# Both heads of an attention unit turned by VectorE, values in mid-step, and the last batch's remainder first

## The chip, the cores and the metric

The kernel runs on one core of a Trainium2 chip. The metric is the time of one execution on the device, in microseconds (us). The core's engines work side by side[...]: TensorE (PE; its weight loads are listed apart as PEld), VectorE (DVE), ScalarE (ACT), GpSimd (POOL), and SyncE (SP), whose queue issues nearly all transfers. Each engine takes its instructions in the order in which the program lists them.

## The reference

Eight batches, eight heads, 576 positions, head dimension 64, all in fp32. Attention keeps the 32 largest scores of every row, and a two-layer network with a normalisation follows on 512 channels:

```python
scores = scale * q @ k^T                      # (B, H, 576, 576)
kth    = 32nd largest of each row
attn   = softmax(scores where scores >= kth, else -1e9)
x      = attn @ v, heads side by side         # (B, 576, 512)
xn     = (x - mean) / sqrt(var + 1e-6) * g_ln
out    = x + relu(xn @ w_ch1) @ w_ch2         # 512 -> 2048 -> 512
```

The two weight matrices arrive as 64-bit floats and are turned to fp32 in the kernel.

## The kernel before, in words

**Units, groups, jobs.** Two heads are worked on together (a head pair, `hp`). A row of 576 positions is cut into four tiles of 128 query rows and a rest of 64. A *unit* is one tile of one head pair, with both heads' rows (two tiles of 128 x 576 scores), or the rest, in which both heads share one tile of 128 rows. There are 160 units: 128 full, 32 rests. A *group* is the units whose results are multiplied with the values in one go, `[0,1]`, `[2,3]`, or with the rest `J` added; a *job* is one group list of one batch and head pair. From batch 2 on a batch has the jobs `[0,1,J]` for its four head pairs, then `[2,3]` for them.

**Steps.** The order is written out by hand: one loop over `n` (line 900) is a step, in which several units stand at different stages. In step n, VectorE selects the top 32 of unit n (`select`, four pieces 0 to 3), while TensorE makes the scores of unit n+1 (`scores`, L354, copied from PSUM by ScalarE in L335), ScalarE masks unit n-1 (`mask`, L442) and exponentiates unit n-2 (`weigh`, L452). Unit n-2 is then *turned*: its weights, queries on partitions, are needed with keys on partitions. The group whose last unit is n-3 is multiplied with the values (`values`, L563 and L570), and `place` transposes the result (L602) and scales it by the reciprocal denominators (L932, L579). Scores live in four buffers used in turn (`scpool`), exponentials in two, the turned weights (`pt`) in one.

**Selection.** A maximum of eight (MAX8) followed by a replacement of those eight (MATCH_REPLACE8), four rounds. From unit 8 on (`EARLY`) units are *halved*: columns i and i + 288 are compared, the larger goes to `hi`, the smaller to `lo`; the 16 largest of `lo` join `hi`, and the four rounds run on 304 columns rather than 576. VectorE makes `hi` (L376); GpSimd makes `lo` as (a + b) - hi on the bit patterns, in L375 and L377. The first eight units run their rounds on whole rows (L416, L423).

**Turning.** Usually four TensorE transposes a head (L505) and a ScalarE copy to `pt` (L517, L521), and one transpose for the last 64 columns of both heads (L538). In 72 units (`moved`: full units from batch 2 on that are not the last of their group) head 1 goes another way: VectorE transposes it in blocks of 32 x 32 (L482) into the unit's own score buffer, one transfer writes that to HBM (L487), and four transfers read it back so that the blocks land on the right partitions of `pt` (L489). `move` stands near the start of the step, after the first piece of the selection.

**The network.** When the x rows of a job list are complete, they become a *block* of two or three tiles of 128 rows (`gives` says at which step). Its work is a list of small TensorE items: transposes of x (L667), the hidden products (L680), the projections (L697). `fill()`, called at eight places of a step, pops items in order, as many as the step's `share` allows; `slot(n)` computes the share so that only `RESERVE` is left when the next block is given. What is left after the last step runs at the end. `dve_cost` and `pe_cost` are the planner's own estimates of a step.

**Start.** Until about unit 16 the weights are converted: ScalarE and GpSimd split and join the 64-bit words, VectorE shifts (L188). `prepare` makes the exponential's bias, on VectorE in this stage (L436, L437) and on GpSimd later.

Of the kernel before, what the change touches and what calls it, by code (L numbers as in the profile page):

```python
# [16 lines left out]
TOP_K = 32  # L17
# [4 lines left out]
J = 4  # L22
# [7 lines left out]
def kernel(  # L30
# [277 lines left out]
    class Unit:  # L308
        def __init__(self, job, group, qt):
            self.job, self.group, self.qt = job, group, qt  # L310
            self.rest = qt == J
            self.tiles = [(0, 1)] if self.rest else [(0,), (1,)]

            self.moved = False

            self.halved = False
            self.e = None
            self.weighed = 0
# [44 lines left out]
    def halve(u):  # L363

        nt = len(u.tiles)  # L370
        u.lo = lopool.tile([P, 2, HALF], FP32, tag="lo", name="lo")
        u.hi = hipool.tile([P, 2, HALF + TOP_K // 2], FP32, tag="hi", name="hi")
        a, b = u.sc[:, 0:nt, 0:HALF], u.sc[:, 0:nt, HALF:S]
        lo, hi = u.lo[:, 0:nt], u.hi[:, 0:nt, 0:HALF]
        nc.gpsimd.tensor_tensor(lo.bitcast(I32), a.bitcast(I32), b.bitcast(I32), ALU.add)  # L375
        nc.vector.tensor_tensor(hi, a, b, ALU.max)  # L376
        nc.gpsimd.tensor_tensor(  # L377
            lo.bitcast(I32), lo.bitcast(I32), hi.bitcast(I32), ALU.subtract
        )

    def select_halved(u, i):
        nt = range(len(u.tiles))
# [22 lines left out]

    def select(u, i):

        if u.halved:
            return select_halved(u, i)
        nt = range(len(u.tiles))  # L410
        if i == 0:
            u.cur = [u.sc[:, t] for t in nt]
            u.wk = {}
        m = small.tile([P, 2, 8], FP32, tag=f"m{i}", name=f"m{i}")
        for t in nt:
            nc.vector.max(m[:, t, :], u.cur[t])  # L416
        if i < TOP_K // 8 - 1:
            for t in nt:
                if i == 0:

                    o = (NF - 4 + 2 * t) * DM
                    u.wk[t] = w2[:].rearrange("p f n -> p (f n)")[:, o : o + S]
                nc.vector.match_replace(u.wk[t], m[:, t, :], u.cur[t], LOWEST)  # L423
                u.cur[t] = u.wk[t]
        if i == 0:
            u.top = m
        u.thr = m

    def prepare(u):

        nt = len(u.tiles)
        u.bias = small.tile([P, 2], FP32, tag="bias", name="bias")
        b = u.bias[:, 0:nt]

        engine = nc.vector if u.i < CONVERTING else nc.gpsimd
        engine.tensor_tensor(b, u.thr[:, 0:nt, 7], u.top[:, 0:nt, 0], ALU.subtract)  # L436
        engine.tensor_scalar(b, b, scale, 0.0, ALU.mult, ALU.add)  # L437

# [27 lines left out]
    def place_of(u):  # L466

        g = u.group  # L470
        if g.pt is None:
            g.pt = ptpool.tile([P, 2 * J + 1, GQ], FP32, tag="pt", name="pt")
            g.ptB = g.pt[:, J : 2 * J].rearrange("p c n -> p (c n)").rearrange(
                "p (i c n) -> p i c n", c=J, n=32
            )
        return sum(P for x in g.qts if x < u.qt)

    def move(u):

        i0 = place_of(u) // 32  # L480
        t = u.sc[:, 1, 0:JP]
        nc.vector.transpose(  # L482
            t.rearrange("p (j c n) -> p j c n", j=P // 32, c=J),
            u.e[:, 1, R:S].rearrange("p (c j k) -> p j c k", c=J, k=32),
        )
        hbm = hbmpool.tile([P, JP], FP32, tag="turned", name="turned")
        nc.sync.dma_start(hbm[:], t)  # L487
        for j in range(P // 32):
            nc.sync.dma_start(  # L489
                u.group.ptB[j * 32 : (j + 1) * 32, i0 : i0 + P // 32].rearrange(  # L490
                    "k i c n -> k i (c n)"
                ),
                hbm[:, j * P : (j + 1) * P].rearrange("(i k) x -> k i x", k=32),
            )

    def turn(u):

        g = u.group
        q0 = place_of(u)
        i0 = q0 // 32  # L500

        def part(t):
            ps = turned()
            for c in range(J):
                nc.tensor.transpose(  # L505
                    ps[:, c * P : (c + 1) * P], u.e[:, t, c * P + t * R : (c + 1) * P + t * R],
                    ident[:],
                )
            if u.rest:
                both = ps[:].rearrange("p (c h n) -> p h c n", h=2, n=R)  # L510
                nc.scalar.copy(g.pt[:, 0:J, q0 : q0 + R], both[:, 0])
                nc.scalar.copy(
                    g.ptB[:, i0 : i0 + R // 32],
                    both[:, 1].rearrange("p c (i n) -> p i c n", n=32),
                )
            elif t == 0:
                nc.scalar.copy(  # L517
                    g.pt[:, 0:J, q0 : q0 + P], ps[:].rearrange("p (c n) -> p c n", n=P)
                )
            else:  # L520
                nc.scalar.copy(  # L521
                    g.ptB[:, i0 : i0 + P // 32],
                    ps[:].rearrange("p (c i n) -> p i c n", c=J, n=32),
                )
# [15 lines left out]

        heads = [0] if u.moved else range(len(u.tiles))
        return [lambda t=t: part(t) for t in heads] + [last]
# [15 lines left out]
    def values(g):  # L558
        vb = g.job.v
        av = brief("av")  # L560
        for c in range(J):
            for h in range(2):
                nc.tensor.matmul(  # L563
                    av[h * D : (h + 1) * D, 0 : g.nq],
                    vb[:, h * J + c, :],
                    g.ptB[:, 0 : g.nq // 32, c, :] if h else g.pt[:, c, 0 : g.nq],
                    start=(c == 0),
# [179 lines left out]
    for b in range(B):  # L747
        parts = [[0, 1], [2, 3], [J]]
        if b:
            parts = [[0, 1], [2, 3]]  # L750
            parts[b < 2].append(J)
        for qts in parts:
# [22 lines left out]
    EARLY = jobs[NHP].first  # L775
    for u in units[EARLY:]:
        u.halved = True

# [36 lines left out]
    SLOTS = 8  # L815
    RESERVE = 4.0
    last_give = max(gives)
# [9 lines left out]

    DVE_UNIT, DVE_REST, DVE_HALVED, DVE_MOVE = 10.3, 5.3, 0.9, 0.8

# [6 lines left out]
    def pe_cost(n):  # L836
# [4 lines left out]
        if ex:  # L841
            c += 0.67 if ex.rest else 0.55 if ex.moved else 1.0
        if g:
# [3 lines left out]
    def dve_cost(n):  # L847
        u, ex = at(n), after(n)[0]
        c = 5.0 if u is None else DVE_REST if u.rest else DVE_UNIT
        if u and u.halved:  # L850
            c *= DVE_HALVED
        return c + DVE_MOVE if ex and ex.moved else c

    def give(n):
# [9 lines left out]
    def slot(n):  # L864


        if n <= CONVERTING:
            return max(0.0, dve_cost(n) - pe_cost(n)) / SLOTS
        left = sum(t[1] for t in todo)
        if n > last_give:  # L870
            even = left / max(1, END - 1 - n)
        else:
            even = 99.0
            for m in sorted(gives):
                if m > n:
                    even = min(even, (left - RESERVE) / (m - n))
                    left += sum(b.cost() for b in gives[m])
        return max(0.0, even) / SLOTS

# [15 lines left out]
    load(fresh[1], nc.sync, nc.scalar)  # L895
    scores(units[0])
    load_gain()
    weights(-1, 0)
    weights(-1, 1)
    for n in range(END):  # L900
# [14 lines left out]
        moved = ex is not None and ex.moved  # L915
        order = (1, 0) if moved else (0, 1)
        sent, stores[:] = stores[:], []

        if ex and not early:
            weigh(ex, order[0])  # L920
        if nxt:
            scores(nxt)
        if g:
            values(g)
        if u:
            select(u, 0)
        if moved:
            move(ex)
        for store in sent:
            store()  # L930
        for den in recips.pop(n, []):
            nc.vector.reciprocal(den, den)  # L932
        if n == gives_first:
# [11 lines left out]
        if ex and len(ex.tiles) > 1 and not early:  # L945
            weigh(ex, order[1])
        fill()
        if parts and not moved:
            parts[0]()
        if ex and ex.rest:  # L950
            keep_den(ex)
        if u:
            select(u, 1)
        if nxt and nxt.halved:
            halve(nxt)
        if n in turns:
            turn_heads(turns[n])
            later = fresh.index(turns[n]) + 1
            if later < len(fresh):
                load(fresh[later], nc.sync, nc.sync)  # L960
        for blk, i in rows_of.pop(n, []):
            blk.stats(i)
        if not quick:
            weights(n, 1)
        fill()
        if mk and not early:
            mask(mk, int(mk.moved))
        if g:
# [4 lines left out]
        fill()  # L973
        if moved:
            parts[0]()
        elif len(parts) > 2:
            parts[1]()
        if u:
            select(u, 2)
        for blk in gives.get(n - 2, []):  # L980
            blk.inverse()
# [10 lines left out]
        if mk and len(mk.tiles) > 1 and not early:  # L992
            mask(mk, 1 - int(mk.moved))
        fill()
# [11 lines left out]
        if u:  # L1006
            select(u, 3)
            if u.i < CONVERTING:
                prepare(u)
        for x in (g, quick):  # L1010
            if x and x.job.hp == NHP - 1:
# [44 lines left out]
```

## Time and profile before

Three runs: 1665.63, 1666.67 and 1667.17 us. The profiled execution has a span of 1666.8 us.

| engine | busy us | share | instructions |
|---|---|---|---|
| TensorE | 1574.1 | 94% | 7113 |
| VectorE | 1464.5 | 88% | 4476 |
| ScalarE | 1077.2 | 65% | 2759 |
| GpSimd | 664.0 | 40% | 879 |

| what | line | count | mean us | busy us |
|---|---|---|---|---|
| projections | L697 | 1152 | 0.599 | 546.1 |
| hidden products | L680 | 2048 | 0.411 | 550.0 |
| transposes of weights | L505 | 864 | 0.285 | 138.1 |
| maxima of halves | L376 | 152 | 0.913 | 138.8 |
| POOL's two passes | L375, L377 | 304 | 1.3 | 394.5 |
| VectorE's move | L482 | 72 | 0.698 | 50.3 |
| write to HBM, 256 KB | L487 | 72 | 2.0 to landing | |
| read back, 64 KB | L489 | 288 | 2.0 to landing | |

Records of TensorE overlap, so busy time is less than count times mean. In the views used below, a line of the timeline has start, length, engine, source line, operation, tile written and read, shapes and count; the square bracket is idle time before it and what ended it. A line of stretches has the busy time of PE, PEld, DVE, ACT and POOL, then the granted clock of TensorE, the share of the transfer engines and GB/s. A line of waits says who waited for whom, in us, how often, and the longest.

### The profile page before, as it was taken

What the parts mean: (1) busy time and instruction counts of PE and PEld (TensorE: products, weight loads), DVE (VectorE), ACT (ScalarE), POOL (GpSimd) and SP (SyncE); (2) the same over time, 40 slices, a digit from 0 to 9 for tenths busy, and PEclk for the clock granted to TensorE, in tenths of its full rate; (3) what the DMA queues carried; (4) which work ended last, traced back from release to release, by engine and by line L of the source; (5) the groups of instructions that cost most, each with busy time, mean ns of one, the idle gap of its engine ahead of it and who ended that gap; (6) DMA issues with size and microseconds to landing.
All of it is one profiled execution on the core that took longest, in us unless ns stands there. A gap on an engine that the chain in (4) does not pass through costs nothing.

```text
span 1666.8 us, 25284 instructions
## 1 busy us (share of the span) xinstructions
PE 1574.1 (94%) x7113; PEld 955.1 (57%) x7113; DVE 1464.5 (88%) x4476; ACT 1077.2 (65%) x2759; POOL 664.0 (40%) x879
## 2 busy tenths in 40 slices
PE   3568989989999999999999999999999999999998
PEld 1346556566555575755547575745547575755564
DVE  5998999999999999999999999899998999998000
ACT  5677967767666776767666675767666676665310
POOL 5567854343433434343343434343243433333010
PEclk9758999999999999999999999999999999999999
DMA  7423333001331133213231233112331132111000
GB/s 176 100 64 108 89 58 59 22 14 27 76 81 51 53 76 81 65 54 69 59 86 51 55 73 83 52 54 70 65 89 44 53 81 74 52 46 47 26 13 13
DMA packets 301203, 104.58 MB, mean 63 GB/s; under 512 B 246276, under 2 KB 283144, under 8 KB 301064
## 3 DMA queue, kind: packets, MB, share of 16 engines
q1 hardware_dynamic: 296328, 102.39, 24.4%
q10 hardware_dynamic: 4736, 0.59, 0.3%
q8 instruction: 57, 0.93, 0.2%
q14 instruction: 82, 0.67, 0.1%
HBM read 74.58 MB, written 28.31 MB: 62 GB/s over the span
## 4 chain that ended last, share of the span: by engine, by line
PE 71%; DVE 21%; issue 4%; ACT 2%; POOL 1%; DMA 1%; ACTq 0%; POOLq 0%; DVEq 0%; SPq 0%
PE hps L680 25%; PE ops L697 24%; PE scps L354 8%; PE av L563 6%; DVE m L398 5%; DVE hi L385 4%; PE tp L505 4%; DVE hi L390 2%; DVE m L416 2%; PE av L570 2%; DVE w L423 2%; DVE lo L385 1%; DVE hi L376 1%; DVE size L188 1%; PE tp L667 1%
## 5 line engine op out<-in xcount | busy, mean ns | idle before, releaser
L680 PE MATMUL hps<-xT,w 128*128 128x256 f32 (+1 forms) x2048 | 550.0, 411 | 2.7 <-ACT xT L672 2.3
L697 PE MATMUL ops<-w,h 128*128 128x512 f32 x1152 | 546.1, 599 | 0.0
L398 DVE MAX8 m<-hi 128x8 f32<-128x304 f32 x1088 | 460.7, 458 | 2.3
L680 PEld LDWEIGHTS hps<-xT,w 128*128 128x128 f32 x2048 | 372.1, 191 | 108.5 <-issue 17.3
L385 DVE MATCH_REPLACE8 hi<-m,hi 128x304 f32<-128x304 f32 x816 | 368.0, 456 | 0.0
L375 POOL TENSOR_TENSOR lo<-sc 128x576 int32<-128x576 int32 (+1 forms) x152 | 197.7, 1301 | 316.3 <-ACT sc L335 156.9
L697 PEld LDWEIGHTS ops<-w,h 128*128 128x128 f32 x1152 | 200.2, 191 | 169.9 <-issue 164.6
L377 POOL TENSOR_TENSOR lo<-lo,hi 128x576 int32<-128x576 int32 (+1 forms) x152 | 196.8, 1295 | 141.9 <-DVE hi L376 139.7
L354 PE MATMUL scps<-kT,qT 64*128 64x288 f32 (+3 forms) x1344 | 217.4, 433 | 32.4 <-DVE qT L304 20.9
L335 ACT COPY sc<-scps 128x288 f32<-128x288 f32 x576 | 199.2, 409 | 62.3 <-PE scps L354 51.0
L442 ACT ACTIVATE e<-sc,m 128x576 f32<-128x576 f32 x288 | 224.3, 779 | 9.7 <-DVE m L398 6.2
L452 ACT ACTIVATE e<-e,bias 128x576 f32<-128x576 f32 x288 | 224.6, 780 | 2.9 <-DVE bias L437 2.5
L390 DVE MAX8 hi<-lo 128x8 f32<-128x288 f32 x544 | 221.8, 443 | 2.6 <-POOL lo L377 1.5
L354 PEld LDWEIGHTS scps<-kT,qT 64*128 64x128 f32 (+1 forms) x1344 | 122.4, 181 | 146.6 <-issue 56.2
L505 PEld LDWEIGHTS tp<-ident,e 128*128 128x128 f32 x864 | 110.9, 147 | 115.9 <-ACT e L452 51.7
L505 PE MATMUL tp<-ident,e 128*128 128x128 f32 x864 | 138.1, 285 | 38.2 <-ACT e L452 37.9
L692 ACT ACTIVATE h<-hps 128x256 f32<-128x256 f32 (+1 forms) x256 | 105.9, 414 | 96.5 <-PE hps L680 93.8
L436 POOL TENSOR_TENSOR bias<-m,m 128x2 f32<-128x2 f32 (+1 forms) x143 | 27.8, 195 | 303.6 <-DVE m L398 303.6
L563 PE MATMUL av<-pt,vb 128*64 128x256 f32 (+2 forms) x1088 | 146.7, 413 | 0.0
L376 DVE TENSOR_TENSOR hi<-sc 128x576 f32<-128x576 f32 (+1 forms) x152 | 138.8, 913 | 5.5 <-ACT sc L335 5.5
L385 DVE MATCH_REPLACE8 lo<-hi,lo 128x288 f32<-128x288 f32 x272 | 118.2, 440 | 0.0
L517 ACT COPY pt<-tp 128x512 f32<-128x512 f32 x128 | 74.6, 583 | 62.1 <-PE tp L505 60.5
(79 smaller groups left out, 1295.0 us busy)
## 6 DMA issues: line engine op xcount, KB each, us to landing
turned<-sc SPq DMA_DIRECT2D x72, 256.0 KB, 2.0
pt<-turned SPq DMA_DIRECT2D x288, 64.0 KB, 2.0
vb<-in_v_dram SPq DMA_DIRECT2D x136, 128.0 KB, 2.5
raw<-in_moe_w_ch_dram SPq DMA_DIRECT2D x32, 512.0 KB, 4.0
kin<-in_k_dram SPq DMA_DIRECT2D x128, 72.0 KB, 2.5
qin<-in_q_dram SPq DMA_DIRECT2D x120, 72.0 KB, 2.5
out_dram<-o SPq DMA_DIRECT2D x32, 256.0 KB, 2.2
ends<-in_v_dram SPq DMA_DIRECT2D x136, 16.0 KB, 2.2
```

The costliest lines, as they stand in the source:

```text
L335: nc.scalar.copy(u.sc[:, t, s * HALF : (s + 1) * HALF], made[s][t][:, 0:HALF])
L354: nc.tensor.matmul(ps[i * R : i * R + ql, o : o + width], qT[r, q0 : q0 + ql], kT[r, k0 : k0 + width], start=True, stop=True,)
L375: nc.gpsimd.tensor_tensor(lo.bitcast(I32), a.bitcast(I32), b.bitcast(I32), ALU.add)
L385: nc.vector.match_replace(x[:, t], m[:, t, :], x[:, t], LOWEST)
L390: nc.vector.max(u.hi[:, t, o : o + 8], u.lo[:, t])
L398: nc.vector.max(m[:, t, :], u.hi[:, t])
L442: nc.scalar.activation(u.e[:, t], u.sc[:, t], AF.Prelu, bias=u.thr[:, t, 7:8], scale=-1.0, alpha=SLOPE)
L452: nc.scalar.activation(u.e[:, t], u.e[:, t], AF.Exp, bias=u.bias[:, t : t + 1], scale=-scale / SLOPE, accum_out=g.den[:, col : col + 1],)
L505: nc.tensor.transpose(ps[:, c * P : (c + 1) * P], u.e[:, t, c * P + t * R : (c + 1) * P + t * R], ident[:],)
L563: nc.tensor.matmul(av[h * D : (h + 1) * D, 0 : g.nq], vb[:, h * J + c, :], g.ptB[:, 0 : g.nq // 32, c, :] if h else g.pt[:, c, 0 : g.nq], ...
L680: nc.tensor.matmul(ps["h"][:, 0:N], w1[:, c, f * P : (f + 1) * P], xT[0][:, c, 0:N], start=(c == 0), stop=(c == NC - 1),)
L697: nc.tensor.matmul(ps[i][:], hT[f][:, i * P : (i + 1) * P], w2[:, f, :], start=(f == 0), stop=(f == NF - 1),)
```

## The change

1. `move` now turns both heads of a moved unit: two VectorE transposes, one transfer of 512 KB to HBM, four transfers back whose runs are 1 KB rather than 512 B. `pt` holds both heads in blocks of 32 queries for this. No head of a moved unit is turned on TensorE; only the last 64 columns are. `move` stands at the end of the step.
2. `values` moves from the start of the step to its middle, the reciprocals of the denominators from the start to after the halving.
3. Every unit is halved, and GpSimd's two passes are (a - hi) + b, so both follow VectorE's maximum.
4. In the converting stage the bias is one VectorE instruction a tile rather than two a unit.
5. The last batch has the jobs `[J]`, `[0,1]`, `[2,3]`, so its rest is worked first and makes a block of one tile. With that, 68 units are moved.
6. The planner: new cost figures, a reserve of 7 rather than 4, and a share proportional to VectorE's cost around the step. Rows' statistics (L629) run later in the step. Moved units mask and weigh head 0 first, as others do.

```diff
@@ halve
-        nc.gpsimd.tensor_tensor(lo.bitcast(I32), a.bitcast(I32), b.bitcast(I32), ALU.add)
         nc.vector.tensor_tensor(hi, a, b, ALU.max)
         nc.gpsimd.tensor_tensor(
-            lo.bitcast(I32), lo.bitcast(I32), hi.bitcast(I32), ALU.subtract
+            lo.bitcast(I32), a.bitcast(I32), hi.bitcast(I32), ALU.subtract
         )
+        nc.gpsimd.tensor_tensor(lo.bitcast(I32), lo.bitcast(I32), b.bitcast(I32), ALU.add)
@@ prepare
-        engine = nc.vector if u.i < CONVERTING else nc.gpsimd
-        engine.tensor_tensor(b, u.thr[:, 0:nt, 7], u.top[:, 0:nt, 0], ALU.subtract)
-        engine.tensor_scalar(b, b, scale, 0.0, ALU.mult, ALU.add)
+        if u.i < CONVERTING:
+            for t in range(nt):
+                nc.vector.tensor_scalar(
+                    b[:, t : t + 1], u.thr[:, t, 7:8], u.top[:, t, 0:1], scale,
+                    ALU.subtract, ALU.mult,
+                )
+            return
...
@@ move
-        t = u.sc[:, 1, 0:JP]
-        nc.vector.transpose(...)
-        hbm = hbmpool.tile([P, JP], FP32, tag="turned", name="turned")
-        nc.sync.dma_start(hbm[:], t)
+        blocks = u.sc[:].rearrange("p t n -> p (t n)")[:, 0 : 2 * JP]
+        for t in range(2):
+            nc.vector.transpose(
+                blocks.rearrange("p (j t c n) -> p j t c n", j=ni, t=2, c=J)[:, :, t],
+                u.e[:, t, t * R : t * R + JP].rearrange("p (c j k) -> p j c k", c=J, k=32),
+            )
+        hbm = hbmpool.tile([P, 2 * JP], FP32, tag="turned", name="turned")
+        nc.sync.dma_start(hbm[:], blocks)
+        for j in range(ni):
...
+                hbm[:, j * 2 * P : (j + 1) * 2 * P].rearrange("(i k) x -> k i x", k=32),
@@ turn
-        heads = [0] if u.moved else range(len(u.tiles))
+        heads = () if u.moved else range(len(u.tiles))
@@ jobs
             parts = [[0, 1], [2, 3]]
-            parts[b < 2].append(J)
+            if b == B - 1:
+                parts = [[J]] + parts
+            else:
+                parts[b < 2].append(J)
@@ planner
-    for u in units[EARLY:]:
-        u.halved = True
-    RESERVE = 4.0
+    RESERVE = 7.0
-    DVE_UNIT, DVE_REST, DVE_HALVED, DVE_MOVE = 10.3, 5.3, 0.9, 0.8
+    DVE_UNIT, DVE_REST, DVE_MOVE, DVE_TURN = 8.6, 5.0, 1.4, 1.45
+        return max(0.0, ratio * pace(n) - pe_cost(n)) / SLOTS
@@ the step
-        if g:
-            values(g)
         if u:
             select(u, 0)
-        if moved:
-            move(ex)
...
-        for den in recips.pop(n, []):
-            nc.vector.reciprocal(den, den)
...
         fill()
+        if g:
+            values(g)
         if parts and not moved:
             parts[0]()
...
         if u:
             select(u, 1)
-        if nxt and nxt.halved:
+        if nxt:
             halve(nxt)
+        for den in recips.pop(n, []):
+            nc.vector.reciprocal(den, den)
...
             select(u, 3)
             if u.i < CONVERTING:
                 prepare(u)
+        if moved:
+            move(ex)
```

## The prediction

> **What bounds the kernel now.** I read the page's slices first, then four stretches, then the waits of VectorE (DVE), then the timeline of PE and DVE.
>
> ```profile
> PE   3568989989999999999999999999999999999998
> ...
> DVE  5998999999999999999999999899998999998000
> ```
>
> Each digit is a busy share in tenths of 41.7 us. In the first eleven slices (to some 458 us) PE has gaps, and DVE hardly any after the first. Then both are full, and DVE stops at about 1542 us while PE works on to the end. Start, us, span, then PE, PEld, DVE, ACT, POOL busy:
>
> ```profile
> 0.00:458.00 458.00, 372.69 (x1788) 235.47 (x1789) 431.15 (x1248) 328.89 (x824) 246.72 (x288) 0.91 0.30 72
> 458.00:1338.00 880.00, 878.16 (x3986) 522.77 (x3986) 842.44 (x2631) 589.36 (x1528) 335.18 (x474) 1.00 0.26 65
> 1338.00:1542.00 204.00, 203.45 (x940) 128.00 (x937) 187.53 (x590) 131.03 (x344) 72.76 (x105) 1.00 0.22 59
> 1542.00:1667.00 125.00, 119.80 (x404) 68.85 (x403) 3.42 (x10) 27.94 (x65) 9.34 (x13) 1.00 0.06 18
> ```
>
> Early (0 to 458) is DVE's: PE idles 85 us. In the middle (batches 2 to 6) PE idles 1.8 us of 880 and DVE 37.6. The end (last batch and tail, 329 us) is PE's. What DVE waits for:
>
> ```profile
> DVE sc L482 <- ACT e L452: 59.4, 19, 13.4
> ```
>
> The move (L482) stands early in its step and waits for an exponential, which follows PE; this is DVE's whole slack. Is PE dense, or only marked busy?
>
> ```profile
> 1443.43 0.60 PE L505 MATMUL tp<-ident,e 128*128 128x128 f32 x4
> ...
> 1604.67 1.04 PE L667 MATMUL tp<-ident,x 128*128 128x128 f32 x8
> ...
> 1606.44 27.89 PE L680 MATMUL hps<-xT,w 128*128 128x256 f32 x128
> 1634.17 27.63 PE L697 MATMUL ops<-w,h 128*128 128x512 f32 x64
> ```
>
> Dense: 64 records in 27.63 us are 0.432 us each, and between 458 us and the end starts of L697 stand 0.440 us apart on average. Four more transposes cost 1.04 - 0.60 = 0.44 us, 0.11 each. A block of two tiles costs PE 1.04 + 27.9 + 27.6 = 56.6 us.
>
> **What the Trainium skill says.** "Perfetto Trace Analysis", Identifying the Most-Contended Engine, calls matmul busy share a poor measure of TensorE; hence the spacing above, which here agrees with the busy share. "SBUF — State Buffer", SBUF: two separate sides: a VectorE instruction with two SBUF inputs and a GpSimd instruction exclude each other for a whole instruction, and the second blocks. The trace agrees:
>
> ```profile
> 1111.09 1.41 POOL L375 TENSOR_TENSOR lo<-sc 128x576 int32<-128x576 int32 x1 [3.22 <-ACT sc L335]
> ...
> 1111.21 1.90 DVE L376 TENSOR_TENSOR hi<-sc 128x576 f32<-128x576 f32 x1
> ...
> 1502.40 0.75 DVE L376 TENSOR_TENSOR hi<-sc 128x576 f32<-128x576 f32 x1
> ```
>
> Begun 0.12 us into POOL's add, the maximum takes 1.90 us; alone, 0.75. "VectorE: DVE Perf Modes", The three transpose paths: VectorE transposes only 32x32 blocks, so the rest of the turn has to be transfers, as here.
>
> **The change, part by part.**
>
> *PE.* 72 units lose head 1's transposes already; now 68 (12 in each of batches 2 to 6, 8 in the last, where [0,1] no longer contains the rest) lose head 0's too. In the middle 57 moves x 4 x 0.11 = -25 us: 855 us of PE work are left. The copies behind them (L517, 0.583 us each on ACT) go as well; ACT is at 67% there, worth nothing by itself.
>
> *DVE, transposes.* L482 runs 72 times at 0.698 us; now 136. Middle: +57 x 0.694 = +39.6 us.
>
> *DVE, halving.* POOL now subtracts only after DVE's maximum, so POOL's first pass can no longer hold the port against it. In the middle L376 is 94 instructions with 88.6 us; 75 full ones at 0.746 and 19 half ones at 0.445 would be 64.4. -24.2 us. Lower bound of the gain: a third, if other POOL work (L638, L710) takes its place; upper: all. I take all, since those ran before, too. The price: both POOL passes (2 x 1.41) follow the maximum. What waits for them is the next step's first maxima of lo; between lie the last two selects (about 4.0 us), so about 1 us is left, and 1.4 more in moved steps. Zero, at most 10 us in all from late POOL queues.
>
> Middle sum for DVE: 842.4 - 24.2 + 39.6 = 858 us, PE 855. Two engines of equal load where there were 880 and 842.
>
> *The move's new place.* At the end of the step its exponentials are long done: the wait at L482 (30.7 us of it in the middle) goes. But the next step's scores go into the same score buffer (four buffers, unit n+1 on that of n-3), and now must wait until the 512 KB have left it. Before, almost a whole step lay between. Counted from the transposes' end:
>
> ```profile
> 1450.49 0.69 DVE L482 STREAM_TRANSPOSE sc<-e 128x512 f32<-128x512 f32 x1
> ...
> 1451.21 0.35 SPq L487 DMA_DIRECT2D turned<-sc  x1
> ...
> 1453.39 1.76 SPq L489 DMA_DIRECT2D pt<-turned  x4
> ```
>
> The readback waits for the landing, 2.2 us after the issue. Each of 16 engines moves eight packets; those of 2 KB took 0.089 us, those of 4 KB (weights) 0.159 median, 0.213 mean, so 512 KB land 0.6 to 1.0 us later: 2.6 to 3.0 us after issue. Then ACT's four copies (1.3 to 1.5 us): scores stand at 3.9 to 4.5 us. DVE wants them at L376, 3.93 us into its step (on the timeline a step's first maximum of lo starts at 1507.91, its L376 at 1511.84). Stall 0 to 0.6 us a move; with ACT ready I take 0.2: 57 x 0.2 = 11 us. Queued behind on ACT are relus (L692), for which three PSUM buffers stand between, so PE runs on. On SP the move follows the loads and the value loads of its step and stands ahead of the next stores; the four readbacks (before 1.76 us to issue) must land before values two steps later, over 10 us: nothing. 1 KB runs make their packets half as many per byte; the doubled bytes raise DMA from 26% to some 35%: nothing.
>
> *Values in mid-step.* Price between 0 and 0.6 us a group: PE's xo transposes need ACT's copy of av (0.43 us), and now only one filler slot lies between rather than three. A slot gives 0.5 to 0.9 us of work. I take 0.05 x 64 = 3 us. Reciprocals after L376 wait for nothing and stand before place: 0.
>
> *Early stage.* Eight units halved: whole rows take 4 x 1.33 + 3 x 1.45 = 9.7 us (pairs of L416 and L423 on the timeline), halved 2.3 + 5.6 + 0.75 = 8.6: -8 us, as DVE binds. POOL gains 8 x 2.85 us in a stage where it is half busy; from -8 to +6 if the joins of weights slip. The bias in one instruction a tile: L436/L437 on DVE have 10.7 + 1.1 + 3.1 us; a fused small one is not shown, 0.17 to 0.67 us by nearest rows: -9 to +7, I take -4. Port: -4 after 208 us. Three moves: +2. Sum about -13, and I take -12.
>
> *End.* The last batch's rest comes first: its block is one tile alone. With 128 columns, 64 hidden products are 128 records; at 0.155 us estimated (256 columns took 0.218, weights' loads 0.191) against 0.107 as share of three tiles: +6 us (0 to +11). Four groups more in values: +3. 16 fewer transposes: -2. The new reserve of 7 leaves 3 us to the end at most. What PE has left when DVE ends shrinks from 3/7 of three tiles (36 us) + 56.6 to some 15 (three short steps and the reserve) + 56.6, but PE is full either way, so only its sum counts: +8.
>
> **The sum.** Middle: DVE 858 + 11 of stall + 3 for values = 872, -8. Early -12, end +8. 1666.8 - 12 - 8 + 8 = 1654.8, so 1655. The profiled span is 1666.8, the runs' median 1666.67, so no shift.
>
> **Rivals.**
> - *PE stays the bound and all its saving shows.* For: gap-free starts before, DVE's slack of 37.6 us. Against: DVE at 858 of 858. Middle 858: 1666.8 - 12 - 22 + 8 = 1641.
> - *The score buffer decides (slower).* At 0.55 us a move the middle is 858 + 31 + 3 = 892, and 1666.8 - 12 + 12 + 8 = 1675; break-even is 0.4 us, and a landing as late as the 512 KB weight loads' (4.0 us on the page, a read) makes it 1.4 us: 1723. For: the 4 KB packets' upper figure, and any other transfer in flight; against: writes of 256 KB were steady at 2.0. Taken at 0.7 us: 1683.
> - *No change.* The place of values costs PE 0.3 us in 56 groups, 17 us, and eats the rest: 1666. Against: ACT waited for av 64 times (119 us), so it is early.
> - *The change does not do what it says*: it can't well, as the transposes at PE vanish with the code; only four of 72 moves go.
>
> **How the numbers follow.** Forecast 0.46, first rival 0.22, second 0.19, third 0.13. Under 0.2% (3.3 us) no difference can be told here. Faster: 0.41 + 0.22 + 0.05 = 0.68. Same: 0.04 + 0.06 = 0.10. Slower: 0.01 + 0.19 + 0.02 = 0.22. The likeliest by itself spans 1643 to 1666; the range, 1630 to 1682, takes in the first rival with 11 us more from the early stage, and about half of the second.
>
> **What would show it.** L505 at some 610 records; L482 136 times, without a wait. L376 at 0.75 us throughout. Middle: DVE over 98% with PE idle 10 us or more (forecast), or PE gap-free (first rival). Second rival: DVE waits at L376 for ACT's sc, and ACT at L335 for the transfer of sc, tens of us. Third: PE idle at L602 for oT. Wrong in the early stage: L390 waiting for POOL's lo.

## The result, and the profile after

The changed kernel takes 1676.31 us (median of four runs, 1676.14 to 1677.18); the kernel before, on the same chip, 1666.92 (1665.63 to 1667.95). The ratio is 1.0058, 95% interval 1.0040 to 1.0075: 9.4 us slower, where 1655 was forecast. The profiled execution spans 1675.4 us.

Line numbers are those of the kernel that a view is of. In the changed kernel the scores are L352 and their copies L333, the maximum of the halves L373, GpSimd's passes L374 and L377, the move L466 with its write L471 and readback L474, the transposes of the weights L488, the values L542 and L549, the copy of their result (`oT`) L554, its transpose in `place` (`xo`) L581, the statistics of the x rows L608, their centring L617, and their transposes for a block L646.

The slices again, on the page of the changed kernel:

```profile
PE   2569989899899999999999999999999999999998
...
DVE  5998999999999999999999999998889878889500
```

TensorE looks as full as before. VectorE, which was at 9 in nearly every slice until it stopped at 1542 us, has slices of 8 and 7 from the 28th on (1130 us), and stops later. The four stretches with the edges of the prediction (columns as there):

```profile
0.00:458.00 458.00, 364.78 (x1751) 227.71 (x1751) 426.12 (x1328) 325.93 (x817) 269.63 (x302) 0.90 0.31 74
458.00:1338.00 880.00, 871.62 (x3754) 500.25 (x3754) 834.76 (x2620) 545.51 (x1445) 329.49 (x468) 1.00 0.35 97
1338.00:1542.00 204.00, 201.63 (x1043) 130.09 (x1043) 174.76 (x557) 126.45 (x343) 68.73 (x101) 1.00 0.28 72
1542.00:1676.00 134.00, 127.21 (x514) 82.80 (x510) 33.84 (x108) 44.08 (x113) 19.70 (x27) 0.99 0.12 38
```

In the same 880 us of the middle, PE has 8.4 us idle rather than 1.8. VectorE has fallen to 834.8 busy, 95%; only short stretches are full (31.00 of 31 us from 552 on). Its waits, largest first, and the one for GpSimd's `lo`:

```profile
DVE hi L373 <- ACT sc L333: 79.7, 55, 5.8
DVE hi L389 <- POOL lo L377: 13.1, 12, 3.0
```

The first is the wait that the second rival named. But 55 us of it lie in the last two batches, and most of that comes with the new order of the last batch: 47 us there with the old planner, 19 with the old order (experiments 6 and 7), none with the new planner alone on the kernel before (experiment 9). PE's own waits:

```profile
PE tp L488 <- ACT e L434: 35.6, 14, 10.8
...
PE tp L646 <- POOL x L617: 13.2, 8, 5.2
PE xo L581 <- ACT oT L554: 12.7, 14, 2.8
PE tp L646 <- POOL r L617: 9.1, 2, 7.4
```

The first is the start (37.9 before). The other three were 5.3, 0.5 and 0.

**Where the time went.** I cut the trace at the first score product of each batch, and priced every TensorE record at the closest spacing of its kind (a projection 0.429 us, a hidden product of 256 columns 0.216, of 128 columns 0.111, a transpose 0.109): that is TensorE's *own work*. The rest of a batch's length is *lost*: waits, changes of tile shape (some 0.2 us where hidden products follow scores, in batch 4), a lower granted clock. Before / after, us:

| batch | length | own work | lost |
|---|---|---|---|
| 0 and 1 | 391.4 / 384.4 | 252.1 / 248.7 | 139.2 / 135.6 |
| 2 | 182.4 / 191.1 | 168.8 / 164.4 | 13.6 / 26.6 |
| 3 | 188.7 / 191.8 | 177.8 / 173.7 | 10.9 / 18.1 |
| 4 | 188.3 / 186.5 | 179.5 / 174.0 | 8.9 / 12.5 |
| 5 | 190.2 / 191.5 | 179.7 / 178.6 | 10.4 / 12.9 |
| 6 | 188.5 / 212.1 | 179.7 / 196.6 | 8.9 / 15.4 |
| 7 and tail | 329.2 / 310.0 | 312.3 / 287.0 | 16.8 / 23.0 |

Own work fell by 27 us in all, and what is lost rose by 35. Batch 2 lost most. Two stretches of it, and the row that PE waits for:

```profile
424.00:456.00 32.00, 24.21 (x84) 12.14 (x85) 31.31 (x96) 15.58 (x42) 12.36 (x20) 0.84 0.37 102
456.00:488.00 32.00, 32.00 (x137) 17.30 (x136) 26.39 (x81) 18.86 (x48) 12.59 (x18) 1.00 0.38 102
```

```profile
447.45 0.69 DVE L608 BATCH_NORM_STATS2 st<-r 128x6 f32<-128x512 f32 x1
...
448.74 0.70 POOL L617 TENSOR_SCALAR r<-r,less 128x512 f32<-128x512 f32 x1
...
449.49 1.11 PE L646 MATMUL tp<-ident,r 128*128 128x128 f32 x4 [7.41 <-POOL r L617]
```

PE has run out of work of the earlier block; the first row of the next one gets its statistics late (L608), is centred late (L617), and PE stands still for 7.4 us. The granted clock in these 32 us is 0.84. In the kernel before, PE was busy for 29.8 us of the same 32, at 0.95.

### The profile page after: what moved, and what is told of

It reads as the page before. It is cut to its first block, busy times and chain, and to the rows that moved or that the text cites. A ratio compares the mean times of both kernels' runs of the same rounds, so it can differ in the third digit from the quotient of the medians.

```text
span 1675.4 us, 25027 instructions
## 1 busy us (share of the span) xinstructions
PE 1565.2 (93%) x7057; PEld 940.8 (56%) x7057; DVE 1469.5 (88%) x4611; ACT 1042.0 (62%) x2715; POOL 687.5 (41%) x897
## 4 chain that ended last, share of the span: by engine, by line
PE 61%; DVE 27%; issue 5%; POOL 4%; ACT 2%; DMA 1%; ACTq 0%; POOLq 0%; DVEq 0%
PE hps L659 22%; PE ops L676 21%; DVE m L397 8%; DVE hi L384 7%; PE scps L352 7%; PE av L542 5%; DVE hi L389 4%; DVE lo L384 2%; DVE hi L373 2%; PE tp L488 2%; PE av L549 2%; DVE size L188 1%; POOL lo L374 1%; POOL lo L377 1%; PE tp L646 1%
## 5 line engine op out<-in xcount | busy, mean ns | idle before, releaser
L659 PE MATMUL hps<-xT,w 128*128 128x256 f32 (+2 forms) x2176 | 551.2, 397 | 2.4 <-ACT xT L651 1.9
L397 DVE MAX8 m<-hi 128x8 f32<-128x304 f32 x1152 | 489.7, 462 | 3.3
L374 POOL TENSOR_TENSOR lo<-sc,hi 128x576 int32<-128x576 int32 (+1 forms) x160 | 209.2, 1307 | 587.7 <-DVE hi L373 298.8
L389 DVE MAX8 hi<-lo 128x8 f32<-128x288 f32 x576 | 234.4, 444 | 14.2 <-POOL lo L377 13.1
L333 ACT COPY sc<-scps 128x288 f32<-128x288 f32 x576 | 198.6, 411 | 70.9 <-PE scps L352 49.2
L352 PE MATMUL scps<-kT,qT 64*128 64x288 f32 (+3 forms) x1344 | 217.2, 431 | 25.4 <-DVE qT L304 22.1
L377 POOL TENSOR_TENSOR lo<-lo,sc 128x576 int32<-128x576 int32 (+1 forms) x160 | 206.7, 1292 | 12.6
L352 PEld LDWEIGHTS scps<-kT,qT 64*128 64x128 f32 (+1 forms) x1344 | 121.9, 180 | 134.4 <-issue 69.0
L373 DVE TENSOR_TENSOR hi<-sc 128x576 f32<-128x576 f32 (+1 forms) x160 | 115.6, 723 | 79.8 <-ACT sc L333 79.7
L671 ACT ACTIVATE h<-hps 128x256 f32<-128x256 f32 (+2 forms) x272 | 109.1, 402 | 100.3 <-PE hps L659 98.4
L542 PE MATMUL av<-pt,vb 128*64 128x256 f32 (+2 forms) x1152 | 146.2, 397 | 0.0
L488 PE MATMUL tp<-ident,e 128*128 128x128 f32 x608 | 97.1, 285 | 35.6 <-ACT e L434 35.6
L488 PEld LDWEIGHTS tp<-ident,e 128*128 128x128 f32 x608 | 77.9, 148 | 83.4 <-ACT e L434 44.4
L542 PEld LDWEIGHTS av<-pt,vb 128*64 128x64 f32 x1152 | 75.2, 141 | 75.9 <-ACT sc L333 22.2
L554 ACT COPY oT<-av 128x256 f32<-128x256 f32 (+2 forms) x72 | 26.9, 374 | 139.3 <-PE av L549 139.2
```

The costliest lines, as they stand in the source:

```text
L352: nc.tensor.matmul(ps[i * R : i * R + ql, o : o + width], qT[r, q0 : q0 + ql], kT[r, k0 : k0 + width], start=True, stop=True,)
L374: nc.gpsimd.tensor_tensor(lo.bitcast(I32), a.bitcast(I32), hi.bitcast(I32), ALU.subtract)
L377: nc.gpsimd.tensor_tensor(lo.bitcast(I32), lo.bitcast(I32), b.bitcast(I32), ALU.add)
L389: nc.vector.max(u.hi[:, t, o : o + 8], u.lo[:, t])
L397: nc.vector.max(m[:, t, :], u.hi[:, t])
L488: nc.tensor.transpose(ps[:, c * P : (c + 1) * P], u.e[:, t, c * P + t * R : (c + 1) * P + t * R], ident[:],)
```

## The experiments

Every ratio is against the kernel before on the same chip, with its 95% interval; "us" is the ratio's difference from 1 times 1666.9, so the changed kernel stands at +9.7. Most intervals are 1 to 2 us to either side.

**1. POOL's passes behind the maximum, alone.** Kernel before plus:

```diff
-        nc.gpsimd.tensor_tensor(lo.bitcast(I32), a.bitcast(I32), b.bitcast(I32), ALU.add)
         nc.vector.tensor_tensor(hi, a, b, ALU.max)
-            lo.bitcast(I32), lo.bitcast(I32), hi.bitcast(I32), ALU.subtract
+            lo.bitcast(I32), a.bitcast(I32), hi.bitcast(I32), ALU.subtract
+        nc.gpsimd.tensor_tensor(lo.bitcast(I32), lo.bitcast(I32), b.bitcast(I32), ALU.add)
```

> The kernel before with one edit: GpSimd's two passes as (a - hi) + b, both behind VectorE's maximum. Theory (VectorE's port wait is what the middle of the changed kernel lives on, but TensorE is the bound before): L376 falls from 139 to about 104 us, yet the time falls only by what VectorE-bound stretches between 208 and 458 us give, 0 to 5 us: 1662 to 1667. Rival (VectorE bounds the middle already): some 20 us faster, 1645. Rival (the later GpSimd pass makes the next step's maxima wait): slower, over 1670, with L390 waiting for lo by tens of us.

1.0012 [1.0006, 1.0019], +2.0 us. Two groups of it (busy us, mean ns, idle time before it):

```profile
L375 DVE TENSOR_TENSOR hi<-sc 128x576 f32<-128x576 f32 x120 | 93.6, 780 | 7.1 <-ACT sc L335 6.6
...
L482 DVE STREAM_TRANSPOSE sc<-e 128x512 f32<-128x512 f32 x72 | 50.4, 701 | 71.9 <-ACT e L452 71.6
```

The maximum falls from 124.6 to 93.6 us, as forecast, and the wait at the move grows from 59.4 to 71.9. Batches 3 to 6 take the same time as before to 0.1 us. VectorE's time is worth nothing there: TensorE sets the pace.

**2 and 3. Both heads moved at the step's end; then with edit 1 too.** Kernel before plus (cut):

```diff
+        for t in range(2):
+            nc.vector.transpose(...)
-        heads = [0] if u.moved else range(len(u.tiles))
+        heads = () if u.moved else range(len(u.tiles))
-        if moved:
-            move(ex)
...
+        if moved:
+            move(ex)
```

> The kernel before with one edit: both heads of the 72 moved units turned by VectorE, the move at the end of the step; values, halving, job order and planner as before. Theory (VectorE becomes the bound): middle 842 + 40 = 882 us of VectorE work against 880 before, so no gain and some stalls: 1667 to 1680. Rival (TensorE stays the bound): its 29 us show, 1640. Rival (the score buffer's handover decides): VectorE waits at L376 for sc by 30 us or more and the time is over 1685.

> The kernel before with both edits together: GpSimd's passes behind the maximum, and both heads moved at the end of the step; early units, values, job order and planner as before. Theory (the middle's sum of 858 for VectorE against 855 for TensorE holds, and the changed kernel lost it again in the early stage and at the end): 1650 to 1660. Rival (the two edits are themselves the loss, by the handover of buffers): 1670 or more, like the changed kernel's 1676.

1.0028 [1.0017, 1.0040] and 1.0034 [1.0022, 1.0046]: +4.7 and +5.7 us. The heart of the change, with only what belongs to it (the layout of `pt`, head 0 masked first, 0.15 us as the planner's price of such a unit on TensorE), makes the kernel slower; the second expectation missed. In the second kernel PE waits for the readback before its values (there L560) 14 times, 24.3 us (experiment 10). In the first, batch 2 takes 188.7 us with some 25 lost, almost as much as in the changed kernel.

**4. First eight units on whole rows again.** Changed kernel, less halving of the first eight units:

```diff
+        if u.i < EARLY:
+            return select_whole(u, i)
...
-        if nxt:
+        if nxt and nxt.i >= EARLY:
             halve(nxt)
```

> The changed kernel, with the first eight units selected on whole rows again. Theory (the early stage gained nothing since GpSimd's 23 us of halving came in the way of the weights' joins): L188 falls back from 28 to about 18 us and the time to 1664 to 1673. Rival (early halving is worth its 8 us of VectorE and something else took the early gain): 1680 to 1686.

1.0043 [1.0031, 1.0055], +7.2 us. That overlaps the changed kernel's interval, so the runs alone show no gain. The profiles agree with a small one: batch 0 takes 209.7 us rather than 213.2 (210.5 to 216.6 in the eight profiles here with early halving), the later batches differ by half a us at most. VectorE's shift of the 64-bit words, in the kernel before, the changed one and this one:

```profile
L188 DVE TENSOR_SCALAR size<-size 128x512 uint32<-128x512 uint32 x32 | 17.8, 590 | 7.3 <-POOL size L185 7.3
```

```profile
L188 DVE TENSOR_SCALAR size<-size 128x512 uint32<-128x512 uint32 x32 | 28.2, 915 | 2.9 <-POOL size L185 2.9
```

```profile
L188 DVE TENSOR_SCALAR size<-size 128x512 uint32<-128x512 uint32 x32 | 19.3, 640 | 6.5 <-POOL size L185 6.5
```

Same instruction, same count: from 0.59 to 0.92 us when POOL halves eight more units, and back to 0.64 without that. Undisturbed it takes 0.39. On the timeline of the changed kernel it lasts 1.62 to 1.64 us seven times, each time begun 0.1 to 0.3 us into a pass of POOL's halving that itself takes some 1.5, and ends 0.3 us after it. Early halving costs VectorE 9 us here (28.2 - 19.3; 5 to 9 over the eight profiles) in waits of this kind, which the prediction didn't count.

**5. One of the two VectorE transposes left out.** Changed kernel; head 0 isn't transposed in `move`, so that part of its weights is left uncomputed:

```diff
-        for t in range(2):
+        for t in (1,):
```

> The changed kernel without head 0's VectorE transposes in the 68 moves (that head's turned weights are then stale data; the transfers stay as they are). Theory (in batches 2 to 5 VectorE is the bound, and what it pays for the turn eats TensorE's saving): 68 x 0.69 = 46 us of VectorE go, batches 2 to 5 fall from 761 us to about TensorE's floor of 4 x 183 = 732, the time to 1640 to 1655. Rival (the handover of the score buffer or the transfers bound the steps, not VectorE's work): no more than 10 us faster, 1666 or more.

1.0012 [1.0004, 1.0020]: 7.6 us less than the changed kernel, for 68 x 0.68 = 46 us less work on VectorE. Batches 4 and 5, of the changed kernel and then of this one:

```profile
775.00:962.00 187.00, 185.86 (x794) 103.33 (x794) 183.28 (x576) 117.86 (x311) 70.23 (x100) 1.00 0.37 100
962.00:1153.00 191.00, 190.04 (x860) 116.20 (x859) 184.74 (x581) 121.63 (x325) 72.35 (x103) 1.00 0.36 99
```

```profile
770.00:956.00 186.00, 184.86 (x790) 102.79 (x786) 175.68 (x561) 116.83 (x309) 70.21 (x100) 1.00 0.37 100
956.00:1148.00 192.00, 191.04 (x865) 116.73 (x866) 178.29 (x571) 122.14 (x328) 72.28 (x103) 1.00 0.36 99
```

VectorE has 6 to 8 us less to do in each, and they take the same 186.5 and 191.5 us (the edges are rounded); TensorE's own work and what it loses are the same too, to 0.1 us. Only batch 3 gains notably, 4.6 us. This is where the forecast's theory of a VectorE bound falls: VectorE at 97% was still not the bound.

**6 to 8. Order of the last batch and planner undone, each and together.** Changed kernel:

```diff
-            if b == B - 1:
-                parts = [[J]] + parts
-            else:
-                parts[b < 2].append(J)
+            parts[b < 2].append(J)
```

```diff
-    RESERVE = 7.0
+    RESERVE = 4.0
...
-                ratio = min(ratio, (left - RESERVE + pe) / dve)
+                even = min(even, (left - RESERVE) / (m - n))
```

> The changed kernel with the last batch's jobs as before, [0,1,J] and [2,3] (72 units moved, no block of one tile). Theory (the one-tile block and four groups more cost TensorE 7 us, where it is the bound): 1668 to 1672. Rival (the shorter tail that the new order gives is worth more than that): 1680 or more.

> The changed kernel with the planner of before (even shares, a reserve of 4, the old cost figures). Theory (the planner only shifts TensorE's work between batches, since VectorE bounds 2 to 5 and TensorE the rest): 1673 to 1679. Rival (the new share overloads batch 6, which takes 212 us against 188 before): 1665 to 1670, with batch 6 at 190 us.

> The changed kernel with both the last batch's jobs and the planner as before. Theory (the order cost 12.6 us and the share 7.3, partly the same overfull batches 5 to 7): 1654 to 1661. Rival (the old share helped only the new order): 1662 to 1667.

Order alone undone: 0.9977 [0.9968, 0.9987], -3.8 us. Planner alone: 1.0010 [1.0002, 1.0018], +1.7. Both: 0.9937 [0.9925, 0.9950], -10.5. So the rest of the change is 10.5 us faster than the kernel before, and these two parts cost 20 us beside it. With both undone, batch 6 takes 186.5 us (212.1 in the changed kernel), and batches 6, 7 and tail together 512.2 rather than 522.1. The rival of the second expectation blames the planner's share for batch 6; but with the planner alone undone batch 6 still takes 207.4 us, with the order alone undone 187.3.

**9. The same two parts, each alone, on the kernel before.** Edits as above, the other way round; in the planner a move is priced at 0.8, as that kernel moves one head.

> The kernel before with one edit: the last batch's jobs are [J], [0,1], [2,3] (68 units moved). Theory (TensorE's own work rises by some 8 us, a block of one tile, four more groups and four unmoved units, and every further block costs it waits at the first transposes): 1675 to 1683, wherever the rest of the change stands. Rival (the order is a loss only beside the new share): 1664 to 1670.

> The kernel before with one edit: the changed kernel's planner (share in proportion to VectorE's cost, reserve 7, its cost figures, with 0.8 for a move). Theory (a share that follows VectorE leaves TensorE short of items in rest steps and at the blocks' change): 1670 to 1678. Rival (it is a loss only where VectorE and TensorE are equally loaded): 1664 to 1669.

Order: 1.0052 [1.0040, 1.0064], +8.7 us, where the prediction had 6 + 3. From batch 5 on, own work grows by only some 3 us, and loss by some 5: a hidden product of the block of one tile stands 0.111 us from the next, not 0.155, so that block costs hardly more than as a share of three tiles, and the sum came out right by luck. The order also puts 18 us more of own work into batch 6, which takes 207.7 us, and takes it from the end. Planner: 1.0048 [1.0036, 1.0060], +8.0 us, where the prediction had 3 at most. Batch 6 doesn't change with it (188.1). It loses 3.3 us in batch 2, where PE now waits 2.8 us for a load of v, and 4.2 in the last batch and tail.

**10. Place of the values and of the statistics.** Values and reciprocals back at the start, on the changed kernel and on that of experiment 8; then, the other way round, values in mid-step on the best kernel of experiment 11, with the reciprocals left where they are (cut):

```diff
+        if g:
+            values(g)
         if u:
             select(u, 0)
...
-        if g:
-            values(g)
```

> The changed kernel with values and the reciprocals back at the start of the step. Theory (in mid-step they cost TensorE 1.5 to 2 us a batch at L581 and in switches, but at the start they would wait for the moved head's transfers, as in the kernel with both edits, 3 to 5 us a batch): 1678 to 1690, TensorE waiting at L542 for pt. Rival (mid-step is where the changed kernel loses): 1662 to 1670.

> The changed kernel with old job order and old planner, and values and reciprocals at the start of the step besides. Theory (at the start values wait for the 128 KB transfers, as in the kernel with only both edits): 1660 to 1668, against 1656 with values in mid-step. Rival (mid-step is a loss of 8 us here too, as it was beside the new order): 1647 to 1652.

> The kernel with 6 of 12 moved units on both heads, with values in mid-step (reciprocals where they were). Theory (there hardly any transfer is late, 2.7 us in all, so mid-step only adds the wait for oT and the switches, 1.5 us a batch): 1652 to 1660 against 1649. Rival (it frees the transfers' wait and the handover at no price): 1643 to 1648.

Back at the start in the changed kernel: 1.0012 [1.0004, 1.0019], +2.0, so mid-step costs 7.7 us there. Back at the start with order and planner as before: 1.0022 [1.0014, 1.0030], +3.7, so mid-step *gains* 14.2. With half as many double moves, mid-step gives 0.9955 [0.9943, 0.9968], 10.7 us more than at the start. Nearly the same edit, three answers. The two kernels with all double moves and values at the start also scatter most (1663.7 to 1673.6 and 1665.9 to 1673.8 us); the profile below is of a run at the lower end. PE's waits at L542 with values at the start, then in mid-step (order and planner as before):

```profile
PE av L542 <- DMA pt<-turned: 24.1, 14, 5.4
```

```profile
PE av L542 <- DMA pt<-turned: 5.8, 6, 1.9
...
PE xo L581 <- ACT oT L554: 8.5, 6, 2.8
```

In the first, one such group's transposes end at 607.8 us, and the four readbacks land at 616.0, 8.3 us on, while values want them earlier. Mid-step takes away most of that wait and brings another, place waiting for ScalarE's copy. In the half-moved kernel little is there to be taken away (2.4 us in 3 waits), and the new wait comes in full (8.5 us in 6). Why it costs in the changed kernel, where the waits for the readback with values at the start are 14.0 us, these sums do not tell; by the profiles the cost lies in batches 6, 7 and tail (522.1 us in mid-step, 511.2 at the start).

The last edit, on the changed kernel, puts the rows' statistics (L608) back where they stood:

```diff
+        for blk, i in rows_of.pop(n, []):
+            blk.stats(i)
...
-        for blk, i in rows_of.pop(n, []):
-            blk.stats(i)
```

> The changed kernel with the rows' statistics back in the middle of the step, before its second half of the selection. Theory (TensorE waits at a block's first transposes for rows that are centred late: 7.7 us in batch 2, 2.0 in batch 3, 4.8 at the end): 1662 to 1669. Rival (VectorE is a step behind by itself and the wait stays): 1674 or more.

1.0039 [1.0025, 1.0052], +6.5 us. That overlaps the changed kernel's interval; the profile shows batch 3 2.2 us shorter, batch 2 hardly.

**11. Fewer double moves.** Kernel before, with POOL's passes as in experiment 1, the bias as in point 4 of the change, `move` at the end, and both heads only in 6 of a batch's 12 moved units, head 1 alone in the others (then, with the second line of the diff, in 8); the planner prices each unit by its heads:

```diff
+            u.heads = (0, 1) if u.qt == 0 or u.qt == 2 and u.job.hp % 2 == 0 else (1,)
+            u.heads = (0, 1) if u.qt == 0 or u.qt == 2 else (1,)
...
-        heads = [0] if u.moved else range(len(u.tiles))
+        heads = [t for t in range(len(u.tiles)) if t not in u.heads]
...
+        if moved:
+            move(ex)
```

> The kernel before with GpSimd's passes behind the maximum, the bias in one instruction a tile while converting, the move at the end of the step, and both heads turned by VectorE in only 6 of the 12 moved units of a batch (the other 6 keep head 1 alone). Theory (a batch takes the longer of TensorE's 188.3 - 0.44 a unit and VectorE's 180 + 0.9 a unit; at 6 units both give 185.6): 13 us from batches 2 to 6, some 5 from the converting stage: 1645 to 1657. Rival (VectorE's small gaps and the late lo cost 7 us a batch from the first unit on): 1664 to 1672.

> As the kernel with 6 of 12 moved units on both heads, but 8 (the first of every job). Theory (there TensorE is still the bound in batches 4 to 6, with no more idle than before): 2 x 0.44 us a batch, 5 us in all: 1642 to 1647. Rival (the transfers of the moves land late for values, or VectorE binds): 1650 to 1660.

Six of twelve: 0.9891 [0.9877, 0.9904], 1649.1 us (1648.1 to 1650.3), 1.1% faster than before and the best of all. Eight of twelve: 0.9903 [0.9890, 0.9917], not told apart from it. Two batches of the kernel with six, again 4 and 5:

```profile
754.00:940.00 186.00, 185.65 (x814) 106.94 (x812) 178.16 (x564) 120.99 (x314) 71.19 (x102) 1.00 0.32 83
940.00:1127.00 187.00, 185.93 (x872) 116.43 (x870) 179.87 (x573) 124.83 (x331) 71.32 (x101) 1.00 0.31 84
```

VectorE keeps 7 to 8 us of slack, and TensorE loses 9.3 and 10.4 us in them, about what it did before the change, with 2.6 us less own work: the saving arrives. The number came out as expected, but not for the reason expected: with eight, VectorE was to bound a batch at 180 + 8 x 0.9 = 187 us, and batch 4 takes 184.8.

9.9 us of the gain come from batch 0, where no unit is moved. POOL's order alone takes 218.4 us there (experiment 1), with the double move and its layout of `pt` besides 216.9 (experiment 3), and this kernel 209.3; what it adds to them in that batch is the bias. That leaves some 8 of the 18 us for the six double moves a batch.

How many units to move depends on the place of values. With values at the start, six of twelve (0.9891) are far faster than twelve (1.0034 in experiment 3, without the bias; 1.0022 in experiment 10, which also halves early and has the statistics later), and PE's waits for the readback are 2.4 us against some 24. With values in mid-step, six (0.9955) are not told apart from twelve with the old order and planner (0.9937).

## Why the prediction was wrong, point by point

- **TensorE loses its transposes: right.** L488 has 608 records (about 610 forecast). All own work fell by 27 us; the sum's terms come to about 18 (25 in the middle, less 7 at the end), as it took the block of one tile too dear.
- **VectorE's transposes: right.** 136 times 0.68 us, with 7.3 us of waits. VectorE's busy time in batches 2 to 5 rose from 720.9 to 735.4 us.
- **Halving frees the port: right in size, worth nothing.** Full maxima fell from 1.04 to 0.78 us. Experiment 1 shows that the time becomes waiting.
- **POOL's later `lo`: priced at zero, at most 10.** It is 13.1 us of VectorE waits in 12 places; VectorE being no bound, only part can matter.
- **The score buffer's handover: right in size.** In batches 2 to 5, 16 of the 48 moves are followed by a wait of over 0.15 us at the next maximum, 6.6 us in all where 0.2 us a move were taken. One of the shorter ones:

```profile
1026.21 0.35 SPq L471 DMA_DIRECT2D turned<-sc  x1
...
1028.95 1.31 ACT L333 COPY sc<-scps 128x288 f32<-128x288 f32 x4 [0.41 <-DMA turned<-sc]
...
1030.29 0.76 DVE L373 TENSOR_TENSOR hi<-sc 128x576 f32<-128x576 f32 x1 [0.20 <-ACT sc L333]
```

  The copies start 2.7 us after the issue (2.6 to 3.0 forecast) and VectorE waits 0.2 us. The second rival ended nearest to the time (1683), but not by its mechanism.
- **Early, -12: mis-sized.** Batches 0 and 1 gained 7.0 us. Halving the first eight units, taken at -8, gains nothing and seems to cost 2 to 4 (experiment 4): the sum counted VectorE's instructions but not L188's waits behind POOL's passes. The bias, taken at -4, looks like -8, near the end of its range (experiment 11). The terms as written also add to -14, not to the -13 and then -12 that were taken.
- **Middle, -8, a step that failed in its mechanism: "Middle sum for DVE: 858 us, PE 855. Two engines of equal load", and the pace set by VectorE.** Experiment 5 shows it: removing 46 us from VectorE frees 7.6. TensorE stayed the bound, as in the first rival, but not free of gaps. Less of its own work came with more loss, 26 us more in batches 2 to 5. The part of that loss that is shown stands in PE's waits there, which rise from 4 to 15 us: rows centred late, place waiting for a copy. A share is tile-shape changes and clock that I have only in sums. The busy share hides such loss: in batch 4 of the kernel before PE is marked busy throughout, and 8.9 of the 188.3 us are lost between records, so the 880 us weren't all work to begin with.
- **Readback, "over 10 us: nothing": wrong by itself.** The data land 8.3 us after the transposes; at the old place of values that costs some 24 us of PE waits beside the old order and planner. Mid-step hides most of it.
- **Values, +3 (third rival 17).** The mechanism of the third rival is there: from 0.5 to 12.7 us of PE, and 33.1 on PE's loads. This is one group:

```profile
1023.39 0.81 PE L549 MATMUL av<-pt,ends 128*128 128x320 f32 x2
...
1024.24 0.43 ACT L554 COPY oT<-av 128x320 f32<-128x320 f32 x1 [2.34 <-PE av L549]
...
1024.71 0.33 PEld L581 LDWEIGHTS xo<-ident,oT 128*128 128x128 f32 x2 [0.48 <-ACT oT L554]
```

  PE finishes av, has too little between, and stands until the copy is done. Measured, the edit is worth from -14 to +11 us by what stands around it, so no single price was right.
- **End, +8, the step that missed by most.** "PE is full either way, so only its sum counts" failed, for both parts. The planner alone costs 8 us with the same sum of work. The order alone costs 8.7, near the 9 that were taken, but only some 3 of it are work, and beside the rest of the change it costs 13.5. The work that the order moves into batch 6 (18 us more there, by experiment 9) and the planner's shares come with waits that a sum doesn't have.

In figures: +9.4 measured against -12 forecast is some 21 us. Order and planner cost 20 beside the rest of the change, where the terms of the end had 10: that is half of it. The rest was to give 22 and gave 10.5. By the profile of experiment 8 it gave 3.9 instead of 12 in the early stage (batches 0 and 1), 2.6 instead of 8 in batches 2 to 6, and 3.5 instead of 2 at the end.

What stays open: by which path batch 2 runs dry. The double move alone brings it (experiment 2: some 25 us lost, where POOL's order alone leaves 14). It stays with the old order and planner (24.2), without one VectorE transpose (190.6 us) and with the statistics at their old place (190.8), and is milder with half the double moves (18.6). So it is neither VectorE's work nor the place of the statistics by itself; no run changed the blocks' supply alone. Open too is why the order costs 13.5 us beside the rest and 8.7 without it.

## What to carry to other kernels

Where two engines are both near full, find out which one binds by taking work off each, before pricing a shift of work between them: here 46 us off VectorE gave 8. Try the shift in parts: with values at the start half of the units gave a gain and all of them a loss, though not because VectorE was full, and with values in mid-step half and all (with the old order and planner) came out alike. An edit that only reorders the binding engine's work (the jobs' order, the planner, the place of a step in the list) has a price of its own, which depends on the other edits, for the place of values even in its sign.

## What the runs showed of the hardware that was not expected

- Recorded lengths of short VectorE instructions differ between kernels at the same pace: MAX8 on 304 columns is recorded at 458 ns before, 462 after and 493 in the best kernel, while starts of neighbouring ones stand 379 to 380 ns apart in all three. A busy sum of such groups is no cost.
- A VectorE instruction on [128 x 1] with two scalars read from memory takes 0.20 us (L413; 0.22 at most, also where it falls inside a two-input pass of POOL, 23 of 33 times); the two-input subtraction on [128 x 2] that it replaces took 0.67 us on average, 0.16 alone.
- The write from SBUF to HBM of 512 KB lands 2.7 us after its issue (median), that of 256 KB 2.0; each of the four readbacks of 128 KB lands after 2.9, of 64 KB after 2.0:

```profile
turned<-sc SPq DMA_DIRECT2D x68, 512.0 KB, 2.7
...
pt<-turned SPq DMA_DIRECT2D x272, 128.0 KB, 2.9
```
